# One expert's first layer begun between attention blocks, and a ring of 15 weight slots in place of 13

## The chip, the cores and the metric

The kernel runs on one core of a Trainium2 chip. The metric is device time in microseconds (us) of the whole kernel; less is better. TensorE (PE) does the matrix products, VectorE (DVE), ScalarE (ACT) and GpSimd (POOL) the element work, and SyncE (SP) issues most of the transfers.

## The reference

An attention of 8 heads (local, masked to a band, plus one on sequences averaged by four), then a mixture of 4 dense experts, then one of 8 experts of which each row takes one:

```python
out_up = np.repeat(out_d, factor, axis=2)                 # attention on averaged q, k, v
out_local = np.matmul(attn, v)                            # banded attention, |i - j| < 4
x = out_up + out_local                                    # 2 x 576 rows of 512

p = domain_probs / (domain_probs.sum(-1, keepdims=True) + 1e-09)
for e in range(4):                                        # dense experts, all 1152 rows
    h = np.maximum(x @ w1[e], 0.0)                        # 512 -> 1024
    out += p[:, e:e + 1] * (h @ w2[e])

expert_idx = np.argmax(logits, axis=1)                    # routed experts
for e in range(8):
    mask = expert_idx == e
    h = np.maximum(x[mask] @ w1[e], 0.0)
    out[mask] = gate_w[mask, None] * (h @ w2[e])
```

## The kernel before, in words

Products are made in two parts of fp32: each weight is split into a high part `wh` (a cast on ACT) and a low part `wl` (a subtraction on DVE), and so are x (`xh`, `xl`) and the hidden layer `hT`. Three matmuls (wh with xh, wh with xl, wl with xh) stand for one product.

**Weights.** The class `Weights` holds the order of all 96 weight tiles (128 x 1024, 512 KB each; a quarter of one expert's w1 or w2). A load (L341, SP's queue) brings a tile into one of a few staging tiles (`raw`), `halves(n)` splits the next n halves of 512 columns (cast L357 on ACT, subtraction L361 on DVE) into a slot of a ring of NSLOT = 13 pairs, and a split tile frees its staging tile for the next load. There are 4 staging tiles up to 480 us; then `late_raw` (4) and two pairs of row blocks of `acc` come to them, which makes 10. Half 0 of a w1 tile holds the parts kk 0 and 1 of the inner dimension, half 1 the parts kk 2 and 3; kk is also the number of the attention unit whose rows of x it meets.

**Attention.** Eight units of two heads each. Units 0 to 3 run alone (0 to about 42 us) in the order of the table `ALONE`: each entry is a step and its delay, so that on every engine steps of several units are interleaved. The steps that matter here: `scores_a`, `scores_b` (L133) and `scores_d` (L150), `exp_*` on ACT, `sum_*` and `scale_*` on DVE and POOL, `turn_*` (transposes L222, L239), `value_a`, `value_b` (L284, the local part) and `value_d` (L271, the averaged part), `add_a`, `add_b` (the two sums x, L299 on DVE), `hi` (xh, L72 on ACT) and `lo` (xl, L318 on DVE). `load_qk` brings k and q of a unit (tile `qk`, three buffers), `load_v` brings two layouts of v (`vg`, averaged, and `vw`, banded; unit 3 has its v in `acc`); `pool_v` sums vg on POOL (L115). Behind `lo` of units 0, 1, 2 one, one and two halves of weights are split.

**First expert.** From about 39 us on, 32 steps take f = 0 to 7 of the hidden layer for two chunks of rows (256 columns in the first): `l1` is 12 matmuls (L473) for one f, its relu is hT (L477 on ACT, L478 on DVE), `l2` is L487. Between the steps units 4 to 7 of the attention run, by the table `BESIDE`. l1 of f = 0 needs xh and xl of units 0 to 3.

**Routed experts.** From about 480 us on. `turn_x` transposes gathered rows and makes gx (L1024, L1025), `layer1` is L1034, `t_half` (L980 transposes, L985 hT on ACT, L986 its low part on DVE), `layer2` L1002 (eight matmuls with the high part of hT, then four with the low one). Each expert is a `body` and, behind a branch on its count of rows, `tiles` (a `small` piece or a further body). Within the body of expert e the calls of `split` split the weights of the expert after it. All engines follow their own instructions in the order of the program; a wait on one of them holds everything behind it there.

## Time and profile before

| | us |
|---|---|
| median of three runs (680.36, 680.80, 685.06) | 680.8 |
| the profiled execution | 676.28 |
| its span, first to last instruction | 674.6 |
| PE busy | 646.6 |
| DVE busy | 345.4 |
| ACT busy | 254.3 |
| POOL busy | 105.5 |
| mean granted clock of PE | 0.992 |

The busy time of an engine is the sum of its instructions; PE's share is the one near the span. Rows of the trace give the start of an instruction from the start of the span, how long it took, engine, line, operation, the tile that it writes and those that it reads, and in brackets how long the engine had stood still before it and for what. Lines are those of the kernel before.

### The profile page before, as it was taken

The page shows a single profiled execution, that of the slowest core. Times are in us where ns is not written, and L with a number is a line of the kernel's source. Part 1 is how long each engine was busy: PE and PEld are TensorE (multiplying, and loading weights), DVE is VectorE, ACT ScalarE, POOL GpSimd, SP SyncE. Part 2 cuts the span into 40 slices and gives each one's busy share as a digit, 9 for nine tenths or more (in the row PEclk, how much of TensorE's full clock was granted, in tenths as well). Part 3 has the DMA queues.
Part 4 walks back from the last instruction along what each step waited for, and adds up shares of the span by engine and source line. Part 5 has one row for each costly group of instructions (what it writes and reads, how often), then busy time and mean ns, then how long its engine had stood idle before and what let it go on. Part 6 is the DMA issues. An engine that isn't in the chain of part 4 may idle for free. (4 is left out here: it accounts for less than half of the span.)

```text
span 674.6 us, 11209 instructions
## 1 busy us (share of the span) xinstructions
PE 646.6 (96%) x4203; PEld 569.3 (84%) x4203; DVE 345.4 (51%) x844; ACT 254.3 (38%) x644; POOL 105.5 (16%) x163
## 2 busy tenths in 40 slices
PE   6889999999999999999999999999999989998996
PEld 5677888999999999999999998899899877787875
DVE  6877753214442132342132347977672269498851
ACT  5646542113331111231111234032642367488752
POOL 6725421100000000000000000403031124121211
PEclk9879999999999999999999999999999999999999
DMA  8916500002430011130011138120861166399600
GB/s 229 290 47 214 180 1 2 2 1 62 118 132 2 1 32 32 63 125 0 1 32 62 64 118 248 41 94 0 302 222 57 34 222 225 137 341 360 219 21 30
DMA packets 25500, 73.58 MB, mean 109 GB/s; under 512 B 3102, under 2 KB 6190, under 8 KB 25408
## 3 DMA queue, kind: packets, MB, share of 16 engines
q1 hardware_dynamic: 23104, 66.12, 29.7%
q0 software_dynamic: 2304, 6.33, 2.9%
q8 instruction: 46, 0.75, 0.5%
q14 instruction: 46, 0.38, 0.2%
HBM read 66.13 MB, written 7.09 MB: 109 GB/s over the span
## 5 line engine op out<-in xcount | busy, mean ns | idle before, releaser
L487 PE MATMUL psb<-wh,hT 128*128 128x512 f32 x576 | 198.4, 396 | 0.8 <-DVE hT L478 0.6
L478 DVE SCALAR_TENSOR_TENSOR hT<-psb,hT 128x384 fp32r<-128x384 f32 (+1 forms) x104 | 54.7, 526 | 223.0 <-ACT hT L477 223.0
L477 ACT ACTIVATE hT<-psb 128x384 fp32r<-128x384 f32 (+1 forms) x104 | 48.6, 467 | 288.1 <-PE psb L473 288.1
L473 PE MATMUL psb<-xh,wh 128*128 128x384 f32 (+1 forms) x416 | 137.0, 329 | 1.5 <-ACT xh L72 1.5
L473 PE MATMUL psb<-xl,wh 128*128 128x384 f32 (+1 forms) x416 | 135.7, 326 | 0.4 <-DVE xl L318 0.4
L473 PE MATMUL psb<-xh,wl 128*128 128x384 f32 (+1 forms) x416 | 135.4, 326 | 0.0
L487 PEld LDWEIGHTS psb<-wh,hT 128*128 128x128 f32 x576 | 108.0, 188 | 22.9 <-DVE hT L478 2.0
L487 PE MATMUL psb<-wl,hT 128*128 128x512 f32 x288 | 113.2, 393 | 0.0
L361 DVE TENSOR_TENSOR wl<-raw,wh 128x512 fp32r<-128x512 f32 x132 | 86.1, 700 | 3.9 <-ACT wh L357 3.3
L473 PEld LDWEIGHTS psb<-xh,wh 128*128 128x128 f32 x416 | 78.7, 189 | 6.2 <-ACT xh L72 1.7
L473 PEld LDWEIGHTS psb<-xl,wh 128*128 128x128 f32 x416 | 78.9, 190 | 4.4 <-DVE xl L318 0.6
L473 PEld LDWEIGHTS psb<-xh,wl 128*128 128x128 f32 x416 | 78.8, 189 | 0.0
L357 ACT CAST wh<-raw 128x512 fp32r<-128x512 f32 x132 | 74.4, 624 | 0.1
L487 PEld LDWEIGHTS psb<-wl,hT 128*128 128x128 f32 x288 | 54.1, 188 | 7.7
L1034 PE MATMUL psb<-wh,gx 128*128 128x256 f32 x288 | 58.2, 289 | 0.1
L615 POOL TENSOR_TENSOR rsq<-ss,nr 128x3 f32<-128x3 f32 x9 | 3.3, 370 | 341.9 <-DVE nr L613 323.7
L1002 PE MATMUL psb<-wh,hT 128*128 128x512 f32 x160 | 53.9, 399 | 0.3 <-ACT hT L985 0.3
L1034 PEld LDWEIGHTS psb<-wh,gx 128*128 128x128 f32 x288 | 46.1, 189 | 2.2 <-issue 1.3
L1034 PE MATMUL psb<-wl,gx 128*128 128x256 f32 x144 | 35.9, 283 | 1.1 <-issue 1.1
L1002 PEld LDWEIGHTS psb<-wh,hT 128*128 128x128 f32 x160 | 30.1, 188 | 6.7 <-ACT hT L985 0.5
L1002 PE MATMUL psb<-wl,hT 128*128 128x512 f32 x80 | 31.5, 394 | 0.0
L1034 PEld LDWEIGHTS psb<-wl,gx 128*128 128x128 f32 x144 | 27.2, 189 | 1.7 <-issue 1.3
(245 smaller groups left out, 790.5 us busy)
## 6 DMA issues: line engine op xcount, KB each, us to landing
raw<-in_moe_w_dram SPq DMA_DIRECT2D x66, 512.0 KB
late_raw<-in_moe_w_dram SPq DMA_DIRECT2D x20, 512.0 KB
acc<-in_moe_w_dram SPq DMA_DIRECT2D x10, 512.0 KB
qk<-in_k_dram SPq DMA_DIRECT2D x8, 288.0 KB
qk<-in_q_dram SPq DMA_DIRECT2D x8, 288.0 KB
rows<-acc SPq DMA_DIRECT2D x9, 256.0 KB
vw<-in_v_dram SPq DMA_DIRECT2D x7, 324.0 KB
vg<-in_v_dram SPq DMA_DIRECT2D x7, 288.0 KB
```

Source lines behind the costliest of these rows:

```text
L357: nc.scalar.copy(hi[:, c], t[:, c])
L361: lo_eng.tensor_tensor(lo[:, c], t[:, c], hi[:, c].bitcast(F32), op=ALU.subtract)
L473: nc.tensor.matmul(t, a[:, kk, fs], b_[:, kk, xs], start=(n == 0), stop=(n == 11))
L477: nc.scalar.activation(out=hi, in_=t, func=AF.Relu)
L478: nc.vector.scalar_tensor_tensor(out=lo, in0=t, scalar=0.0, in1=hi.bitcast(F32), op0=ALU.max, op1=ALU.subtract)
L487: nc.tensor.matmul(ys[t], a[:, ts], b_[:, f % 2, :], start=(f == 0 and j == 0), stop=(f == 7 and j == 2))
L615: eng.tensor_tensor(t, ss, y, op=ALU.mult)
L1002: nc.tensor.matmul(y, gh[:, f, a], b_[:, f % 2, :], start=(n == 0), stop=(n == 23))
L1034: nc.tensor.matmul(dst, a[:, kk], w[:, kk, :], start=(n == 0), stop=(n == 11))
```

## The change

Four things. The loads of k, q of unit 3 go to staging tiles 2 and 3 of the ring and stand at the head of SP's queue, ahead of v of unit 1; v of unit 2 and the first two weights are issued at `pool_v` of unit 0, the next two at `scores_d` of unit 3. The first expert's order of weights begins with w1 c0, w1 c1, w2 c0, w2 c1, and behind `lo` of units 0, 1, 2 one, two and one halves are split. `l1_ahead` opens four tiles (f = 0 to 3) between `value_a` and `value_d` of unit 3 with the parts kk 0 and 1, adds kk 2 behind `value_b`, and `l1` of f = 0 to 3 is left with kk 3. And late in the kernel two more slots come to the ring in place of the four `late_raw` tiles (15 slots, 6 staging tiles), four halves are split ahead of the loop over the routed experts, and the bodies of experts 3 and 4 split 14 halves in place of 16.

```diff
--- before.py
+++ after.py
@@ -75,10 +75,13 @@
 
     def load_qk(self, u, d):
         b, hp = self.units[u]
-        t = self.ld.tile([128, 2, S], F32, tag="qk", name="qk", bufs=3)
-        self.nc.sync.dma_start(out=t[:, 1, :], in_=self.k[b, hp])
-        self.nc.sync.dma_start(out=t[:, 0, :], in_=self.q[b, hp])
-        d["qT"], d["kT"] = t[:, 0, :], t[:, 1, :]
+        if "qk" in self.room.get(u, {}):
+            d["qT"], d["kT"] = self.room[u]["qk"]
+        else:
+            t = self.ld.tile([128, 2, S], F32, tag="qk", name="qk", bufs=3)
+            d["qT"], d["kT"] = t[:, 0, :], t[:, 1, :]
+        self.nc.sync.dma_start(out=d["kT"], in_=self.k[b, hp])
+        self.nc.sync.dma_start(out=d["qT"], in_=self.q[b, hp])
 
     def load_v(self, u, d):
         b, hp = self.units[u]
@@ -331,6 +334,7 @@
         self.index = {key: i for i, key in enumerate(order)}
         self.loaded = self.split = self.half = 0
         self.raws = {}
+        self.grown = 1 << 30
 
     def load_to(self, n):
         while self.loaded < min(n, len(self.order)) and self.raw:
@@ -351,7 +355,7 @@
                 return
             self.load_to(i + 1)
             t = self.raws[i]
-            hi, lo = self.slots[i % NSLOT]
+            hi, lo = self.slot(i)
             c = slice(512 * s, 512 * s + 512)
             if hi_engines[self.half % len(hi_engines)] == "a":
                 nc.scalar.copy(hi[:, c], t[:, c])
@@ -375,8 +379,21 @@
 
     def get(self, key):
         i = self.index[key]
-        assert (self.half + 1) // 2 - NSLOT <= i < self.split, (key, i, self.half)
-        return self.slots[i % NSLOT]
+        assert (self.half + 1) // 2 - len(self.slots) <= i < self.split, (key, i, self.half)
+        return self.slot(i)
+
+    def slot(self, i):
+
+        if i < self.grown:
+            return self.slots[i % NSLOT]
+        n = len(self.slots) - NSLOT
+        r = (i - self.grown) % len(self.slots)
+        return self.slots[NSLOT + r] if r < n else self.slots[(self.grown + r - n) % NSLOT]
+
+    def more_slots(self, slots):
+        assert self.half % 2 == 0
+        self.grown = self.half // 2
+        self.slots += slots
 
 
 def rsqrt(nc, pool, y, ss):
@@ -427,7 +444,9 @@
     srcs = [(w1a[e], w2a[e]) for e in range(E1)] + [(w1b[e], w2b[e]) for e in range(E2)]
     order = []
     for e in range(E1):
-        for c in range(4):
+        if e == 0:
+            order += [(0, w, c) for w in (0, 1) for c in (0, 1)]
+        for c in range(2 if e == 0 else 0, 4):
             order += [(e, 0, c), (e, 1, c)]
     for e in range(E1, E1 + E2):
         order += [(e, 0, c) for c in range(4)] + [(e, 1, c) for c in range(4)]
@@ -461,8 +480,27 @@
         if fill:
             fill.pop(0)()
 
+    opened = {}
+
+    def l1_ahead(fs, kks):
+
+        for f in fs:
+            if f not in opened:
+                opened[f] = bank()[:, 0:256]
+            wh, wl = (t.rearrange("p (k f) -> p k f", k=4) for t in W.get((0, 0, f // 2)))
+            fs_ = slice(128 * (f % 2), 128 * (f % 2) + 128)
+            for kk in kks:
+                for j, (a, b_) in enumerate(((wh, xh), (wh, xl), (wl, xh))):
+                    nc.tensor.matmul(
+                        opened[f], a[:, kk, fs_], b_[:, kk, 0:256],
+                        start=(kk == 0 and j == 0), stop=(kk == 3 and j == 2),
+                    )
+
     def l1(e, c, f):
         t0, nt = CHUNKS[e][c]
+        if e == 0 and c == 0 and f in opened:
+            l1_ahead((f,), (3,))
+            return l1_keep(opened.pop(f), f, nt)
         wh, wl = (t.rearrange("p (k f) -> p k f", k=4) for t in W.get((e, 0, f // 2)))
         fs = slice(128 * (f % 2), 128 * (f % 2) + 128)
         xs = slice(128 * t0, 128 * (t0 + nt))
@@ -473,6 +511,9 @@
                 nc.tensor.matmul(t, a[:, kk, fs], b_[:, kk, xs], start=(n == 0), stop=(n == 11))
                 n += 1
                 between()
+        l1_keep(t, f, nt)
+
+    def l1_keep(t, f, nt):
         hi, lo = hT[:, f % 4, 0, 0:128 * nt], hT[:, f % 4, 1, 0:128 * nt]
         nc.scalar.activation(out=hi, in_=t, func=AF.Relu)
         nc.vector.scalar_tensor_tensor(out=lo, in0=t, scalar=0.0, in1=hi.bitcast(F32), op0=ALU.max, op1=ALU.subtract)
@@ -518,20 +559,29 @@
             nc.gpsimd.memset(t[:, 144:160], 0.0)
         acc_f = acc[0:72].rearrange("p t d -> p (t d)")
         pT = acc_f[:, 2304:4608].rearrange("p (n i c) -> p n i c", n=2, i=9)
-        room = {3: dict(vw=acc_f[:, 0:1152], vg=acc_f[:, 1152:2176])}
+        room = {3: dict(qk=[raws[i][:, 0:S] for i in (2, 3)], vw=acc_f[:, 0:1152], vg=acc_f[:, 1152:2176])}
         att = Attention(nc, cst, ld, wk, bank, q, k, v, xh, xl, [pT[:, i] for i in range(2)], room)
         nc.gpsimd.dma_start(out=pr, in_=probs.rearrange("(t p) e -> p t e", p=128))
         half = H // 2
         W.ahead = 0
-        for name, u in (("load_qk", 0), ("load_qk", 1), ("load_qk", 2), ("load_v", 0), ("load_v", 1)):
-            att.load(name, u)
+        for u in range(3):
+            att.load("load_qk", u)
+        att.load("load_v", 0)
+        att.load("load_qk", 3)
+        att.load("load_v", 1)
+        att.load("load_v", 3)
         for name, u in att.run(att.ALONE, range(half)):
-            if name == "scores_d" and u == 0:
-                for name, u in (("load_qk", 3), ("load_v", 3), ("load_v", 2)):
-                    att.load(name, u)
+            if name == "pool_v" and u == 0:
+                att.load("load_v", 2)
+                W.load_to(2)
+            elif name == "scores_d" and u == 3:
                 W.load_to(NRAW)
             elif name == "lo" and u < 3:
-                W.halves((1, 1, 2)[u], "a", "v")
+                W.halves((1, 2, 1)[u], "a", "v")
+                if u == 2:
+                    l1_ahead(range(4), (0, 1))
+            elif name == "value_b" and u == 3:
+                l1_ahead(range(4), (2,))
         W.ahead = NRAW
         run = att.run(att.BESIDE, range(half, 2 * half))
         rest, done = half * len(att.BESIDE), 2
@@ -968,7 +1018,7 @@
     hs_s = lp.tile([128, FF], F32, name="hs_s")
     yo_s = lp.tile([64, DM], F32, name="yo_s")
     yt_s = lp.tile([64, DM], F32, name="yt_s")
-    raws = [lp.tile([128, 1024], F32, name=f"late_raw{i}") for i in range(4)]
+    W.more_slots(make_slots(lp, 2, NSLOT))
 
     def t_half(h, hs2=None):
 
@@ -1065,10 +1115,10 @@
         deliver()
         split(2)
         layer1(e, 1)
-        split(3)
+        split(2 if e in (3, 4) else 3)
         layer1(e, 2)
         t_half(0)
-        split(3)
+        split(2 if e in (3, 4) else 3)
         layer1(e, 3)
         turn_x()
         layer2(e, 0)
@@ -1176,7 +1226,6 @@
     fixed["ab"] = [bank(), bank()]
     for t in range(3):
         r.store(t)
-    W.more_raw(raws)
     layer1(0, 0)
     for t in range(3):
         r.turn(t)
@@ -1217,6 +1266,7 @@
     load_count(0)
     turn_x()
     fixed["h"][2:] = [bank(), bank()]
+    W.halves(4, HI, LO)
     for e in range(E2):
         if e == 1:
             body_ahead(e)
```

On PE, at the end of the attention units that run alone, before the change: value_a of unit 3 (rows with `acc` alone), value_d, value_b, then l1 of f = 0.

```order
L284 MATMUL psb<-acc 64x64 x8
L271 MATMUL psb<-dT,vd 64x144 x4
L284 MATMUL psb<-acc 64x64 x10
L473 MATMUL psb<-xh,wh_92 128x256
L473 MATMUL psb<-xl,wh_92 128x256
L473 MATMUL psb<-xh,wl_93 128x256
```

And now, where wh_92 is the tile of f = 0 and 1, and wh_94 that of f = 2 and 3:

```order
L287 MATMUL psb<-acc 64x64 x8
L494 MATMUL psb<-xh,wh_92 128x256
L494 MATMUL psb<-xl,wh_92 128x256
L494 MATMUL psb<-xh,wl_93 128x256
...
L494 MATMUL psb<-xh,wh_94 128x256
L494 MATMUL psb<-xl,wh_94 128x256
L494 MATMUL psb<-xh,wl_95 128x256
L274 MATMUL psb<-dT,vd 64x144 x4
L287 MATMUL psb<-acc 64x64 x10
L494 MATMUL psb<-xh,wh_92 128x256
```

24 matmuls of the first layer moved in between value_a and value_d, and 12 begin behind value_b.

On SP's queue, behind k and q of units 0, 1, 2 and v of unit 0, before the change (first vg and vw are of unit 1, `acc` is v of unit 3, the last of unit 2):

```order
L90 DMA vg<-in_v_dram 72x1024
L95 DMA vw<-in_v_dram 72x1152
L79 DMA qk<-in_k_dram 128x576
L80 DMA qk<-in_q_dram 128x576
L90 DMA acc<-in_v_dram 72x1024
L95 DMA acc<-in_v_dram 72x1152
```

And now:

```order
L83 DMA raw_111<-in_k_dram 128x576
L84 DMA raw_110<-in_q_dram 128x576
L93 DMA vg<-in_v_dram 72x1024
L98 DMA vw<-in_v_dram 72x1152
L93 DMA acc<-in_v_dram 72x1024
L98 DMA acc<-in_v_dram 72x1152
```

k and q of unit 3 moved ahead of v of unit 1.

On DVE, ahead of the first branch of the routed experts (L1154 before, L1204 now), before the change and then now:

```order
L1025 TENSOR_TENSOR gx<-psb,gx 128x4x128
L1018 CAST gx<-gx 128x4x64
L1154 COMPARE_AND_BRANCH
L1159 COMPARE_AND_BRANCH
L1132 CAST oidx_s<-meta_t 64x1
```

```order
L1075 TENSOR_TENSOR gx<-psb,gx 128x4x128
L1068 CAST gx<-gx 128x4x64
L365 TENSOR_TENSOR wl_101<-raw_109,wh_100 128x512 x2
L365 TENSOR_TENSOR wl_103<-raw_110,wh_102 128x512 x2
L1204 COMPARE_AND_BRANCH
```

Four subtractions came in ahead of the branch; on ACT four casts stand behind its gx in the same way.

## Rows read from the trace of the kernel before

**Rows 1.** The page: span, busy time, share and instructions of each engine.
```profile
span 674.6 us, 11209 instructions
PE 646.6 (96%) x4203; PEld 569.3 (84%) x4203; DVE 345.4 (51%) x844; ACT 254.3 (38%) x644; POOL 105.5 (16%) x163
```

**Rows 2.** Waits of PE: who for whom; us in total, times, longest.
```profile
PE psb L133 <- DMA qk<-in_q_dram: 2.7, 2, 1.7
PE psb L271 <- ACT dT L72: 1.8, 2, 1.1
```

**Rows 3.** Windows: busy us of PE, PEld, DVE, ACT, POOL; PEclk, DMA share, GB/s.
```profile
19.00:24.00 5.00, 5.00 (x83) 4.03 (x84) 4.40 (x14) 3.14 (x17) 3.64 (x7) 1.00 1.03 252
28.00:32.00 4.00, 3.98 (x37) 3.16 (x39) 3.86 (x11) 4.00 (x17) 1.32 (x2) 0.60 0.89 335
42.16:63.24 21.08, 20.27 (x182) 16.06 (x182) 14.95 (x35) 9.97 (x42) 6.11 (x7) 0.84 0.52 159
```

**Rows 4.** Timeline, 18 to 25 us: start, duration, instruction, idle time before it.
```profile
18.88 0.75 DVE L108 TENSOR_REDUCE qd<-qk 128x144 f32<-128x576 f32 x1 [0.18 <-DMA qk<-in_q_dram]
18.99 0.71 PE L133 MATMUL psb<-qk 64*64 64x68 f32 x16 [1.73 <-DMA qk<-in_q_dram]
23.03 0.53 DVE L202 TENSOR_REDUCE sm<-P 128x5 f32<-128x360 f32 x1 [0.39 <-ACT P L175]
24.98 0.26 DVE L195 TENSOR_SCALAR smd<-smd 128x3 f32<-128x3 f32 x1 [0.99 <-ACT Pd L175]
```

**Rows 5.** Timeline, 35 to 43 us.
```profile
35.53 1.15 DVE L361 TENSOR_TENSOR wl<-raw,wh 128x512 fp32r<-128x512 f32 x1
37.45 0.69 PE L284 MATMUL psb<-acc 68*64 68x64 f32 x16
39.40 1.29 DVE L361 TENSOR_TENSOR wl<-raw,wh 128x512 fp32r<-128x512 f32 x2
40.60 0.82 DVE L299 TENSOR_TENSOR x<-psb,od 128x256 f32<-128x256 f32 x2
42.18 0.38 PE L473 MATMUL psb<-xh,wh 128*128 128x256 f32 x1 [1.45 <-ACT xh L72]
```

**Rows 6.** Timeline of PE: first-layer matmuls, six apart, then ten apart.
```profile
47.57 0.41 PE L473 MATMUL psb<-xh,wl 128*128 128x256 f32 x1
48.85 0.41 PE L473 MATMUL psb<-xh,wl 128*128 128x256 f32 x1
...
57.95 0.28 PE L473 MATMUL psb<-xl,wh 128*128 128x256 f32 x1
59.14 0.28 PE L473 MATMUL psb<-xh,wl 128*128 128x256 f32 x1
```

**Rows 7.** Timeline, 50 to 64 us.
```profile
50.16 0.42 DVE L478 SCALAR_TENSOR_TENSOR hT<-psb,hT 128x256 fp32r<-128x256 f32 x1 [1.72 <-ACT hT L477]
63.29 0.52 PE L239 MATMUL psb<-ident,Pd 128*72 128x128 f32 x3 [0.43 <-DVE hT L478]
```

**Rows 8.** Timeline, 503 to 508 us, and four casts in a run at 614 us.
```profile
503.60 0.58 ACT L1024 CAST gx<-psb 128x512 fp32r<-128x512 f32 x1 [1.07 <-PE psb L1022]
505.43 0.29 DVE L1018 CAST gx<-gx 128x256 fp32r<-128x256 f32 x1
506.04 0.39 PE L1002 MATMUL psb<-wh,hT 128*128 128x512 f32 x1
507.90 1.09 PE L1002 MATMUL psb<-wh,hT 128*128 128x512 f32 x4
...
614.15 2.19 ACT L357 CAST wh<-late_raw 128x512 fp32r<-128x512 f32 x4
```

**Rows 9.** Timeline of PE: where a routed expert's work begins behind a branch.
```profile
598.32 0.63 PE L980 MATMUL psb<-ident,acc 128*128 128x128 f32 x4 [0.71 <-DVEq L1154]
664.77 0.63 PE L980 MATMUL psb<-ident,acc 128*128 128x128 f32 x4 [0.30 <-DVE metap L1226]
```

**Rows 10.** Windows, columns as in rows 3: 40 us of the routed experts.
```profile
590.00:630.00 40.00, 36.89 (x242) 32.18 (x241) 35.37 (x73) 32.54 (x68) 7.47 (x6) 1.00 0.96 348
```

## The prediction

> **What bounds the kernel now.** The page's first rows: TensorE (PE) is busy 646.6 of 674.6 us [rows 1], so time is won only where PE stands still, runs at a low clock, or does less. The list of PE's waits says where it stands still; the waits near this change are 2.7 us for q by DMA (the longest 1.7) and 1.8 us for dT from ScalarE (ACT; the longest 1.1) [rows 2]. The windows give the clock: from 42.16 to 63.24 us the granted clock is 0.84 in the mean; as there are two levels, 1.2 and 2.4 GHz, that is 21.08 x 0.16 / 0.5 = 6.7 us at the lower one [rows 3]. The timeline joins the two: PE stands still for 1.45 us until 42.18, for xh of unit 3 [rows 5], and then works at half clock. A first-layer matmul comes every (48.85 - 47.57) / 6 = 0.213 us there, and every (59.14 - 57.95) / 10 = 0.119 us at full clock [rows 6]. So the change works on two stalls (18.99 and 42.18) and on the slow stretch behind the second; it also puts work ahead of the first routed expert (504 us) and takes some from two later ones (584 to 612 us).
>
> **The head: k, q of unit 3 earlier.** PE waits 1.73 us at 18.99 for q of unit 3, VectorE (DVE) 0.18 us at 18.88 for the same q [rows 4]. On SP's queue k3 and q3 now stand ahead of vg1 and vw1 (72 x 1024 and 72 x 1152 elements of 4 bytes, 0.63 MB), at 252 GB/s [rows 3] 2.5 us. So q3 should land at 18.9 - 2.5 = 16.4, before PE asks for it at 18.99 - 1.73 = 17.26. PE's wait goes. But DVE is nearly without a gap there, and can win its own idle time: 0.18, 0.39 at 23.03 and 0.99 at 24.98, sum 1.56 [rows 4]. Against that stands vg1. Before, vw1, k3 and q3 (0.92 MB, 3.7 us) landed behind it, so it was there at about 15.2; now k3 and q3 (0.59 MB, 2.3 us) come first, so 17.5, and GpSimd (POOL) began its sum over vg1 at 17.21: 0.3 to 0.4 us late, with little slack (busy 3.64 of 5.00 us [rows 3]). I take 1.56 - 0.36 = **-1.2 us**, between -0.2 (vg1, and vg2 behind it, set the pace) and -1.7 (all of PE's wait). The weight loads behind them move by less than 1 us and are cast much later: nothing.
>
> **Tiles ahead: the first expert's first step.** 24 matmuls now stand between the local part of unit 3 (value_a) and its downsampled part (value_d), 12 more behind value_b, and 3 are left in each of the steps f0 to f3, where there were 12. PE's work is the same in all.
> Step by step: value_a ends at 38.14 (37.45 + 0.69 [rows 5]); 24 x 0.119 = 2.9 us bring the start of value_d to 41.0 and the end of value_b, 1.3 us on, to 42.3. The two sums x of unit 3 began at 40.60 and took 0.82 [rows 5]; now the second needs value_b, and ends at about 42.85. xh on ACT (0.67) ends at 43.55 and xl on DVE begins at 43.6, where it began at 42.16: **1.4 us later**. PE meanwhile has its 12 matmuls, 42.3 + 1.4 = 43.7: it isn't idle when xh arrives, so the 1.45 us stall goes; about 0.6 us (43.55 + 0.12 to 44.35) are left for xl. The clock should stay at its upper level: an idle time of 1.73 us at 18.99 was followed by 1.00 from 19 to 24 [rows 3, 4], one of 1.45 us at 42.18 by the slow stretch, so a gap of 0.6 us is a likely pass, no certain one.
> What PE could win by 63 us: 27 matmuls fewer (36 before, less the 9 that it ran early, 3.2 us), and half of 6.7 us (3.4), less 1.4: about 5 us. But DVE has the chain that PE waits for: from xl of unit 3 to hT of f3, 42.16 to 63.24, it is busy 14.95 of 21.08 us [rows 3], and at 63.29 PE waits 0.43 us for that hT [rows 7]. DVE's work there stays the same, for the same number of halves is split before it. From 43.6 on, 14.95 us end at 58.55; to that comes the idle time that is left. Of 6.13 us idle, 1.72 (50.16) came from a PE at half clock [rows 7] and should go, with some 0.4 more of that kind; the rest waits for ACT's exponentials and casts, which start earlier but don't get shorter. I keep 2.0 us: 60.55 against 63.24, **-2.7 us**. If only 2.1 go: 62.6, -0.7; if 0.5 is left: 59.05, -4.2. From 64 to 480 us PE stands still for less than 1 us, so what it has won by then moves the end.
> Held banks: four PSUM banks stay open until f3, so the next output tile of PE shares a bank with unit 4's exponentials on ACT and waits for them. The cover is PE's own lead of 2 us over DVE; I cost it at nothing (without the cover, one group of exponentials, 1.2 us).
> The split half that moves from the third unit to the second lands beside POOL's work. DVE's row at 35.53, beside POOL, took 1.15 us; two at 39.40 took 1.29 together, 0.65 each [rows 5]: +0.5 us of DVE, hidden, as PE's 24 matmuls begin 1.4 us after it. The Trainium skill, GPSIMD Engine Reference, section 1. Specifications, says that GpSimd shares its SBUF interfaces with VectorE and contends with DVE instructions that have two SBUF inputs: it speaks against this place, and the trace agrees, with 1.15 against 0.65 us. Put on the path, it would take 0.5 us off the gain.
>
> **The ring: 15 slots, six staging tiles.** Four halves now stand on ACT and DVE between the last turn of x and the first branch. Four casts take 2.19 us [rows 8]. ACT's gx ends at 504.18 and hT came right behind; now hT starts at 506.4, its first part (0.35) ends at 506.7, and the second layer begins there instead of at 506.04, +0.7. DVE has its cast of gx until 505.72, then four subtractions, 4 x 0.645 = 2.58 us, so 508.3; two copies and the first hT (0.7) end at 509.0, where the low matmuls began at 507.90 [rows 8]: **+1.2 us** with the hand-over. The cover would be other work for PE ahead of this layer, and the order has none. Between 0 and +2.6 (all of DVE's share).
> Experts 3 and 4 split 14 halves where they split 16: 1.1 us less on ACT and 1.3 on DVE in each. PE waits 0.71 us at such a boundary (598.32) for DVE, and 0.30 at the last one (664.77), where the body before split 8 halves [rows 9]. So at most 0.4 a body; I take **-0.4** for both, between 0 and -0.8.
> Staging tiles: 6 instead of 10. The DMA engines run at 0.96 and 348 GB/s from 590 to 630 us [rows 10]; a weight of 128 x 1024 x 4 bytes takes 1.5 us. A body of 13.7 us uses 8 weights, 12 us of DMA, in bursts of one per 1.2 us; six tiles, full at its start, last for it. I cost it at nothing.
>
> **Sum.** -1.2 - 2.7 + 1.2 - 0.4 = -3.1 us. The profiled execution is 676.28 us (span 674.6 [rows 1] and 1.7 around it), so 673.2. It lies 4.5 us under the median of the runs shown, 680.8; against that median the forecast is **677.7 us**.
>
> **Rivals.**
> 1. DVE doesn't hold the gain back. Head -1.7, steps -4.2, ring 0, bodies -0.4: -6.3, **674.5 us**. For it: 6.13 us of idle time in DVE's chain [rows 3]. Against it: most of that waits for ACT, not for PE.
> 2. The clock falls again. PE is ahead of DVE by about 2 us in f0 to f3, so it idles there in gaps, and a gap of 1.1 us (dT [rows 2], just ahead of 28) was followed by 0.60 from 28 to 32 [rows 3]. A low stretch as long as before costs 3.4 us and eats the 2.7: -1.2 + 0.8 = -0.4, **680.4 us**. The Trainium skill, TensorE: Matmul & The Clock Gate, A second HAM failure mode: psum-queue depth-cycling, says that frequent short idle times between groups of matmuls send the clock down and up: by it the gain of the steps would be lost. The trace is divided: 1.73 us of idle time passed at 18.99, 1.45 did not at 42.18.
> 3. The other side: staging tiles. Bodies of experts 3 to 6, 584 to 640 us: six tiles are used up within a body, ACT stands at a cast with hT behind it in its queue, and PE behind hT. Price: 1.5 us for each weight that comes late. One in each of four bodies is +6.0, less 3.1: **683.7 us**; it decides from the third late weight on. For it: DMA at 0.96 [rows 10] has nothing to spare when 8 weights and the gathers are wanted in 13.7 us. Against it: two of the four bodies want a weight less, and with ten tiles no cast waited for a load.
>
> **How the numbers follow.** Forecast (675.8 to 679.5): 0.45. Rival 1: 0.17. Rival 2: 0.25. Rival 3: 0.13. The range, 673.5 to 682.0, reaches past the middle of rival 1 and over rival 2, and leaves out most of rival 3. One per cent, 6.8 us, is about what a measurement of this kernel can tell from no change: faster than 674.0 takes the far part of rival 1, 0.10; slower than 687.6 wants two late weights a body, 0.04; within 1%: 0.86.
>
> **What would show it.** Right: no PE wait for q near 17 to 19 us; PE's wait for xh near 43 under 0.5 us, and the clock at 1.00 from 40 to 62; hT of f3 3 to 4.5 us before 63.24 (head and steps); the second layer of the first routed body 2 to 3 us behind gx; no ACT wait for a DMA past 580 us. Wrong: a clock under 0.9 in 40 to 62, POOL waiting over 1 us for vg near 17, ACT casts that wait for a load in the routed experts.

## The result, and the profile after

| | before | after |
|---|---|---|
| median of the runs taken side by side (20 each), us | 679.97 | 684.48 |
| ratio after / before, 95% interval | | 1.0063, 1.0043 to 1.0083 |
| profiled execution, us | 676.28 | 688.9 |

The changed kernel is slower, by about 4.3 us (0.0063 x 680). The forecast was 677.7 us, the range 673.5 to 682.0. The loss is small, 0.6 per cent, but clear of the noise: the interval leaves out 1.

The first rows of the page after, which answer to [rows 1]:

```profile
span 687.1 us, 11208 instructions
PE 657.9 (96%) x4203; PEld 577.9 (84%) x4203; DVE 347.1 (51%) x844; ACT 255.4 (37%) x644; POOL 100.0 (15%) x163
```

PE does the same 4203 matmuls and is busy 11.3 us longer, so more of its work ran at the lower clock. This is not what separates the medians: the mean granted clock is 0.987 over the 20 executions of the changed kernel and 0.988 over 29 of the kernel before, a difference worth some 0.7 us (0.001 x 680). The profiled execution of after (clock 0.977) is the slowest of its 20. Of the waits of [rows 2] the one for q fell from 2.7 to 0.9 us (its longest part, of 1.7, is gone); the one for dT grew from 1.8 to 2.7 us:

```profile
PE psb L274 <- ACT dT L72: 2.7, 2, 1.6
```

The windows of after (columns as in [rows 3]) show where in the attention part the clock is low:

```profile
34.00:45.00 11.00, 9.85 (x72) 8.15 (x73) 7.11 (x13) 4.70 (x11) 5.27 (x7) 0.54 0.08 30
45.00:60.00 15.00, 14.59 (x180) 11.73 (x178) 8.93 (x25) 7.72 (x29) 1.86 (x3) 1.00 0.39 125
```

In this execution the slow stretch did not go; it moved. Before, it lay behind 42.18 us [rows 3, 5]; now it lies at 34 to 45 us (0.54), ahead of and under the tiles begun early. Two rows of the kernel before (start, duration, engine, line, operation, tiles, idle time ahead of it), then the timeline of after, 32 to 50 us:

```profile
34.19 0.72 PE L271 MATMUL psb<-dT,vd 72*64 72x144 f32 x8 [0.65 <-ACT dT L72]
42.16 0.76 DVE L318 TENSOR_TENSOR xl<-x,xh 128x576 fp32r<-128x576 f32 x1 [0.74 <-ACT xh L72]
```

```profile
32.47 1.09 DVE L198 TENSOR_SCALAR smd<-smd 128x3 f32<-128x3 f32 x1
34.39 0.87 DVE L74 COPY acc<-psb 68x128 f32<-68x128 f32 x2
34.70 0.40 ACT L72 COPY dT<-psb 72x288 f32<-72x288 f32 x1 [2.55 <-DVE acc L74]
35.15 1.23 PE L274 MATMUL psb<-dT,vd 72*64 72x144 f32 x8 [1.61 <-ACT dT L72]
41.07 1.12 PE L287 MATMUL psb<-acc 68*64 68x64 f32 x16
42.12 0.58 PE L494 MATMUL psb<-xh,wh 128*128 128x256 f32 x1
46.26 0.28 PE L494 MATMUL psb<-xh,wl 128*128 128x256 f32 x1
47.61 0.82 DVE L302 TENSOR_TENSOR x<-psb,od 128x256 f32<-128x256 f32 x2 [4.35 <-ACT od L72]
49.18 0.76 DVE L321 TENSOR_TENSOR xl<-x,xh 128x576 fp32r<-128x576 f32 x1 [0.74 <-ACT xh L72]
```

Read from the top: PE waits 1.61 us for dT, where it waited 0.65 before; ACT's dT itself stands 2.55 us behind a copy on DVE. PE then goes on at half clock: value_a of unit 3 ends at 42.19 (forecast 38.14), the 24 matmuls of the tiles ahead stand between 42.12 and 46.54, and DVE has nothing to do for 4.35 us until the sums x can start. xl of unit 3 begins at 49.18; it began at 42.16 before, and 43.6 was forecast.

The timeline of after, 65 to 74 us, where four tiles are closed:

```profile
65.16 0.42 DVE L519 SCALAR_TENSOR_TENSOR hT<-psb,hT 128x256 fp32r<-128x256 f32 x1
65.77 1.27 POOL L118 TENSOR_TENSOR pv<-vg 72x512 f32<-72x512 f32 x1 [4.72 <-DMA vg<-in_v_dram]
67.80 0.91 POOL L212 TENSOR_TENSOR Pd<-Pd,smd 128x432 f32<-128x432 f32 x1
68.76 1.32 PE L242 MATMUL psb<-ident,Pd 128*72 128x128 f32 x6 [1.95 <-POOL Pd L212]
73.11 0.42 DVE L519 SCALAR_TENSOR_TENSOR hT<-psb,hT 128x256 fp32r<-128x256 f32 x1 [1.02 <-ACT hT L518]
```

The first and the last row are hT of f = 3 and f = 4. In the kernel before they are:

```profile
62.83 0.41 DVE L478 SCALAR_TENSOR_TENSOR hT<-psb,hT 128x256 fp32r<-128x256 f32 x1
67.55 0.41 DVE L478 SCALAR_TENSOR_TENSOR hT<-psb,hT 128x256 fp32r<-128x256 f32 x1
```

Between them lie 7.95 us instead of 4.72: POOL waits 4.72 us for vg of unit 4, then scales Pd, and PE waits 1.95 us for Pd (where it waited 0.43 us for DVE [rows 7]). This wait is nowhere in the prediction. Last, two rows of after from the routed experts:

```profile
515.36 0.50 PE L1052 MATMUL psb<-wh,hT 128*128 128x512 f32 x1 [0.38 <-ACT hT L1035]
577.35 1.14 ACT L361 CAST wh<-raw 128x512 fp32r<-128x512 f32 x2 [0.54 <-DMA raw<-in_moe_w_dram]
```

PE waits behind the four halves, as forecast, and a cast waits for its load, as rival 3 said.

### The profile page after: what moved, and what is told of

The parts are those of the page before. It is cut to its first block, busy times and chain, and to the rows that moved or that the text cites. A ratio compares the mean times of both kernels' runs of the same rounds, so it can differ in the third digit from the quotient of the medians.

```text
span 687.1 us, 11208 instructions
## 1 busy us (share of the span) xinstructions
PE 657.9 (96%) x4203; PEld 577.9 (84%) x4203; DVE 347.1 (51%) x844; ACT 255.4 (37%) x644; POOL 100.0 (15%) x163
## 5 line engine op out<-in xcount | busy, mean ns | idle before, releaser
L511 PE MATMUL psb<-xh,wh 128*128 128x384 f32 (+1 forms) x400 | 132.0, 330 | 0.0
L511 PE MATMUL psb<-xl,wh 128*128 128x384 f32 (+1 forms) x400 | 130.8, 327 | 0.0
L511 PE MATMUL psb<-xh,wl 128*128 128x384 f32 (+1 forms) x400 | 130.8, 327 | 0.0
L365 DVE TENSOR_TENSOR wl<-raw,wh 128x512 fp32r<-128x512 f32 x160 | 105.5, 711 | 7.6 <-ACT wh L361 6.7
L361 ACT CAST wh<-raw 128x512 fp32r<-128x512 f32 x160 | 89.4, 624 | 0.6 <-DMA raw<-in_moe_w_dram 0.5
L511 PEld LDWEIGHTS psb<-xh,wh 128*128 128x128 f32 x400 | 75.7, 189 | 4.3 <-issue 0.2
L511 PEld LDWEIGHTS psb<-xl,wh 128*128 128x128 f32 x400 | 75.7, 189 | 3.8
L511 PEld LDWEIGHTS psb<-xh,wl 128*128 128x128 f32 x400 | 75.7, 189 | 0.0
L1084 PE MATMUL psb<-wh,gx 128*128 128x256 f32 x288 | 60.5, 296 | 0.2
L1084 PEld LDWEIGHTS psb<-wh,gx 128*128 128x128 f32 x288 | 47.8, 195 | 2.3 <-issue 1.4
```

The lines of the kernel that those rows point to most:

```text
L361: nc.scalar.copy(hi[:, c], t[:, c])
L365: lo_eng.tensor_tensor(lo[:, c], t[:, c], hi[:, c].bitcast(F32), op=ALU.subtract)
L511: nc.tensor.matmul(t, a[:, kk, fs], b_[:, kk, xs], start=(n == 0), stop=(n == 11))
L1084: nc.tensor.matmul(dst, a[:, kk], w[:, kk, :], start=(n == 0), stop=(n == 11))
```

## The experiments

Each kernel was timed in rounds beside the kernel before, except where noted. Below, "us" beside a ratio is (ratio - 1) x 680.

| kernel | ratio to before, 95% interval | us |
|---|---|---|
| a_only: attention part alone | 1.0038, 1.0011 to 1.0065 | +2.6 |
| b_only: ring part alone | 1.0053, 1.0027 to 1.0079 | +3.6 |
| behind: changed, all early tiles behind value_b | 1.0081, 1.0055 to 1.0107 | +5.5 |
| raw6: six staging tiles alone | 1.0033, 1.0004 to 1.0063 | +2.2 |
| dve_extra: four subtractions done twice | 1.0044, 1.0017 to 1.0071 | +3.0 |
| act_scale: row maxima scaled on ACT | 1.0000, 0.9967 to 1.0032 | 0.0 |
| head_only: loads of k, q of unit 3 first | 1.0005, 0.9975 to 1.0036 | +0.3 |
| ahead_only: early tiles alone | 1.0008, 0.9974 to 1.0041 | +0.5 |
| behind_only: early tiles alone, behind value_b | 1.0035, 1.0004 to 1.0067 | +2.4 |
| fill2: two tiles, behind value_b | 1.0007, 0.9989 to 1.0024 | +0.5 |
| order_only: the order of weights alone | 0.9991, 0.9964 to 1.0019 | -0.6 |
| qk7_before: load order of unit 7 alone | 1.0005, 0.9978 to 1.0032 | +0.3 |
| qk7_a_only | 0.9993, 0.9973 to 1.0013 | -0.5 |
| qk7_after | 1.0047, 1.0024 to 1.0071 | +3.2 |
| qk7_fill2 | 0.9958, 0.9936 to 0.9981 | -2.9 |
| k8_a_only | 0.9986, 0.9959 to 1.0013 | -1.0 |
| k8_fill2 | 0.9954, 0.9923 to 0.9986 | -3.1 |

### The two parts apart, the early tiles moved, and the changed kernel once more

a_only undoes the ring part, b_only the attention part (the four edits of the diff split where the change lists them). `behind` moves the 24 early matmuls:

```diff
-                if u == 2:
-                    l1_ahead(range(4), (0, 1))
             elif name == "value_b" and u == 3:
-                l1_ahead(range(4), (2,))
+                l1_ahead(range(4), (0, 1, 2))
```

> The attention part alone (head loads, order of weights, tiles ahead), with the ring of 13 slots and 10 staging tiles and the splits as before. Theory 1 (24 matmuls ahead of value_d hold up the sums x of unit 3; VectorE idles there some 4 us and is the bound up to about 90 us): slower than before by 2 to 4 us. Theory 2 (the loss comes from the ring and the four halves at 504 us): faster than before by 2 to 4 us, as forecast. Theory 3 (the clock): the time follows the granted clock, 0.98 and less where it is slow.

> The ring part alone (15 slots, six staging tiles, four halves ahead of the routed experts, 14 halves in two bodies), with the attention as before. Theory 1: slower by 0.8 to 2 us, the price put on it in the prediction. Theory 2: slower by 4 us and more. Theory 3: within 1 us of before, as the clock of the first 80 us is that of before.

> The changed kernel, but all 36 matmuls ahead (parts 0, 1 and 2 of four tiles) stand behind value_b of unit 3 and none ahead of value_d. Theory 1: the sums x of unit 3 come as early as before, VectorE has no gap of 4 us, and the kernel is 3 to 5 us faster than the changed one: 0 to 2 us faster than before. Theory 2: as slow as the changed kernel, +4 us. Theory 3: between the two, as the clock falls.

> The changed kernel once more, for a second profile. Theory 1: VectorE again stands idle for about 3 to 4 us ahead of the sums x of unit 3, at whatever clock, and TensorE waits over 1 us for VectorE or GpSimd between 60 and 72 us. Theory 3: the gaps are there only where the clock is at its lower level.

Both parts cost. `again`, the changed kernel executed once more, took 682.27 us (span 680.5, clock 0.987). There, too, DVE stands idle ahead of the sums x of unit 3, with the clock at 1.00 (2.12 us, the row below; nothing before), and PE waits 1.70 us for Pd at 64.90. Behind value_b the early tiles are no cheaper, so their place between value_a and value_d alone does not explain the loss.

```profile
44.02 0.82 DVE L302 TENSOR_TENSOR x<-psb,od 128x256 f32<-128x256 f32 x2 [2.12 <-ACT od L72]
```

What the prediction had taken for a property of the kernel shows in b_only, whose attention part is that of before. The windows from xl of unit 3 to hT of f = 4, each by its own times, of before, b_only, a_only (in this order):

```profile
42.16:67.55 25.39, 24.53 (x213) 19.98 (x214) 18.18 (x43) 13.82 (x56) 8.88 (x11) 0.87 0.55 172
```
```profile
42.22:65.61 23.39, 21.34 (x210) 17.43 (x211) 17.98 (x43) 13.82 (x56) 8.82 (x11) 1.00 0.66 189
```
```profile
46.29:69.13 22.84, 18.23 (x185) 14.28 (x185) 18.24 (x44) 13.93 (x56) 8.79 (x11) 1.00 0.65 191
```

The same stretch in the same order ran at 0.87 in one execution and at 1.00 in another, and was 2.0 us shorter there. With the early tiles it is 0.55 us shorter again, no more: DVE has some 18 us of work in it in all three. And it begins 4.1 us later in a_only. Not all of the four are the price of the early tiles, since xl also comes late without them where the clock fell ahead of it (44.18 in raw6, whose attention is that of before, and 45.08 in order_only). Compared at an equal time at the lower clock ahead of 110 us (3.4 us, one execution each), PE's matmul that starts at 110 us in before comes 1.6 us earlier in b_only and 2.0 earlier in qk7_before, both with the old order of first loads and tiles, but only 0.1 earlier in k8_a_only, which has the early tiles (the qk7 and k8 kernels are described below). At 10.3 us of lower clock before and raw6 stand at 0 and +1.1, again, ahead_only and qk7_after at +1.9, +2.6 and +3.6. So the early tiles bought 0.5 to 1.3 us behind xl, paid some 3 ahead of it in k8_a_only (45.37 against 42.22), and lost 1.5 us or more: near the 2.6 us that a_only measured, but read from single executions.

Four rows of b_only (hT of f = 3 and f = 4, POOL's sum over vg of unit 4, PE's first matmul with Pd) hold two more things:

```profile
59.83 0.41 DVE L517 SCALAR_TENSOR_TENSOR hT<-psb,hT 128x256 fp32r<-128x256 f32 x1
65.61 0.41 DVE L517 SCALAR_TENSOR_TENSOR hT<-psb,hT 128x256 fp32r<-128x256 f32 x1
58.06 1.29 POOL L118 TENSOR_TENSOR pv<-vg 72x512 f32<-72x512 f32 x1 [3.12 <-DMA vg<-in_v_dram]
61.41 0.85 PE L242 MATMUL psb<-ident,Pd 128*72 128x128 f32 x6 [1.63 <-POOL Pd L212]
```

With the attention of before, hT of f = 3 ends here at 60.24, earlier than the 60.55 that was forecast of the changed kernel. And POOL's wait for vg is there without any early tile: it was hidden in the profiled execution of before, whose DVE came later.

### The ring part: which of its edits costs

raw6 is the kernel before with six staging tiles in place of ten, and nothing else:

```diff
-    raws = [lp.tile([128, 1024], F32, name=f"late_raw{i}") for i in range(4)]
...
-    W.more_raw(raws)
```

> The kernel before with its four late staging tiles left out: six instead of ten, and nothing else. If staging tiles are what the ring part costs (rival 3): slower by 2 to 3.6 us, with ACT casts or TensorE waits later than before in the routed experts. If its cost is the four halves at 504 us and the new order behind them: within 0.7 us of before.

It costs 2.2 of the part's 3.6 us. Its timeline (ACT, ACT, PE):

```profile
571.22 0.62 ACT L357 CAST wh<-raw 128x512 fp32r<-128x512 f32 x1 [1.67 <-DMA raw<-in_moe_w_dram]
571.74 0.64 ACT L984 CAST hT<-psb 128x256 fp32r<-128x256 f32 x2
572.16 0.50 PE L1001 MATMUL psb<-wh,hT 128*128 128x512 f32 x1 [0.86 <-ACT hT L984]
```

ACT stands at a cast whose load has not landed, hT stands behind it in ACT's queue, and PE waits for hT. Lining up PE's matmuls of the two kernels, raw6 falls 1.4 us back from 570 to 579 us and another 1.0 by 669. In the kernel before no cast waits for a load in this stretch. The other kernels say how much such a comparison of two executions is worth: from 560 to 581 us of the kernel before, the thirteen others with ten staging tiles lie within 0.3 us of it, and the five with the whole ring part fall 0.5 to 1.1 back (2.6 in qk7_after, with a stretch at the lower clock). From 499 to 507 us, where the four halves stand, those five lose 0.7 to 0.9 us (b_only 0.9), all others 0.0 or less. In the four of them that were executed more than once the time is also 0.2 to 0.4 us longer outside the span from first to last instruction, and no trace shows why.

### DVE's load, and the head alone

dve_extra repeats the subtraction of four halves on DVE (halves 8 to 11 of the order); act_scale takes the scaling of the row maxima (TENSOR_SCALAR, x -scale) from DVE and multiplies on ACT; head_only makes only the edit to the first loads.

```diff
-            lo_eng.tensor_tensor(lo[:, c], t[:, c], hi[:, c].bitcast(F32), op=ALU.subtract)
+            for _ in range(2 if self.half in (8, 9, 10, 11) else 1):
+                lo_eng.tensor_tensor(lo[:, c], t[:, c], hi[:, c].bitcast(F32), op=ALU.subtract)
```
```diff
-        self.nc.vector.tensor_scalar(out=m, in0=m, scalar1=-scale, scalar2=None, op0=ALU.mult)
+        self.nc.scalar.mul(d["mx"][:, 0:4], d["mx"][:, 0:4], -0.125)
...
+        self.nc.scalar.mul(d["mx"][:, 4:9], d["mx"][:, 4:9], -0.125)
...
+        self.nc.scalar.mul(d["mxd"], d["mxd"], -0.125 / 16)
```

> The kernel before with four subtractions wl done twice (halves 8 to 11, 60 to 67 us): 4 x 0.68 = 2.7 us more work on VectorE, the same result. Theory D (VectorE is the bound there): slower by 2 to 3 us. If TensorE is the bound there, as the prediction had it behind 64 us: within 0.7 us of before.

> The kernel before, with the scaling of the row maxima (24 small instructions on VectorE, 0.17 us each alone, 0.4 to 1.9 us beside GpSimd's work; 7.9 us in all) moved to ScalarE, just ahead of the exponentials. Theory D: faster by 2 to 5 us, as VectorE loses 7.9 us in the first 112 us. If TensorE is the bound: within 1 us of before.

> Only the head of the change: k, q of unit 3 at the head of SP's queue (and the loads behind them moved with them); weights, tiles and ring as before. Theory D (VectorE, held up by GpSimd, sets the pace from 17 to 78 us): TensorE's wait of 1.7 us at 19 us goes, comes back as a wait of over 2 us for dT near 34 us, and the kernel is within 1 us of before. The prediction's step: 1.2 us faster. Theory C (the idle time near 34 us lowers the clock): 1 to 2 us slower, with a mean clock lower by 0.002 or more.

2.6 us more of DVE cost 3.0 us (0.0017 x 680 = 1.2 at the least), though PE's rows line up with a loss of only 0.8 of it from 59 to 71 us, where the work was added, and the profiled execution was at the lower clock for some 19 us more than that of before (0.978 of 686.4 us, 0.992 of 674.6); it agrees with a DVE that sets the pace and settles nothing. act_scale moves nothing measurable, against the 2 to 5 us of theory D (beside GpSimd's work these instructions took 0.3 to 1.3 us in before, not up to 1.9). The head gains nothing measurable either. Its timeline:

```profile
18.05 0.71 PE L136 MATMUL psb<-raw,raw 64*64 64x68 f32 x16
26.41 2.13 DVE L162 TENSOR_SCALAR mx<-mx 128x5 f32<-128x5 f32 x1
34.32 0.88 DVE L74 COPY acc<-psb 68x128 f32<-68x128 f32 x2
35.08 1.24 PE L274 MATMUL psb<-dT,vd 72*64 72x144 f32 x8 [2.08 <-ACT dT L72]
```

PE's wait for q is gone, as forecast (first row; [rows 4] has 1.73 us). But DVE did not win its idle time: a scaling of five columns now falls beside a sum on POOL and takes 2.13 us (0.72 before, at 26.94; 0.83 in after), and DVE's copy of unit 2 comes at 34.32, later than the 33.43 of before. PE, early, waits the longer for dT. What sets the time of that copy shows in the sums of POOL over v of unit 2, of before and of after:

```profile
23.95 1.26 POOL L115 TENSOR_TENSOR pv<-vg 72x512 f32<-72x512 f32 x1 [0.47 <-DMA vg<-in_v_dram]
24.90 1.27 POOL L118 TENSOR_TENSOR pv<-vg 72x512 f32<-72x512 f32 x1 [0.92 <-DMA vg<-in_v_dram]
```

From the start of this sum to DVE's copy lie 9.5 us in both (33.43 and 34.39), in head_only (24.84 to 34.32) and in twelve other traces, to within 0.02 us. So POOL, which has waited for v in most of them, paces this stretch, and DVE follows. The new loads bring PE there earlier, and POOL not: in head_only and after its sum starts 0.9 us later than before, in `again` 0.4 earlier.

### The attention part's edits apart

```diff
             elif name == "value_b" and u == 3:
+                l1_ahead(range(2), (0, 1, 2))
```

That is fill2: of f = 0 and 1 the parts kk 0 to 2 stand behind value_b, 18 matmuls where 9 stood. ahead_only has the early tiles as changed but no new first loads; behind_only the same with all of them behind value_b; order_only only the order of the weights and no early tile.

> Only the tiles ahead, with the order of weights that they need (head loads and ring as before): 24 matmuls ahead of value_d of unit 3, 12 behind value_b. The prediction's step: 2.7 us faster. Theory D (VectorE sets the pace from 17 to 78 us, and these matmuls make the sums x of unit 3 some 3 us late): 1.5 to 3 us slower.

> As ahead_only, but all 36 matmuls stand behind value_b of unit 3. The sums x are in time, the first relu is 1.5 to 2 us later than before. Theory D: 0.5 to 2 us slower, less than ahead_only. The prediction's sum with nothing late on VectorE: 2.7 us faster or more.

> The kernel before, with 18 matmuls (parts 0, 1, 2 of f = 0 and 1, for which its own order of weights is enough) behind value_b of unit 3: 9 that stood there already, and 9 that fill most of TensorE's 1.45 us wait at 42 us. Nothing on VectorE is later than before, and the second relu comes earlier. Theory D: 0 to 1.5 us faster, as VectorE's wait of 1.7 us at 50 us shrinks. If idle time at 42 us is what lowers the clock: also a higher mean clock by 0.002.

> Only the order of the first expert's weights and the halves behind lo of units 0, 1, 2 (1, 2, 1 in place of 1, 1, 2), without tiles ahead. The moved subtraction lands beside GpSimd's work (1.15 us in place of 0.65). Theory D: 0 to 0.7 us slower. If the order itself is the loss: 2 us slower and more.

None gains, and their intervals overlap, so these runs do not tell which edit of the attention part costs. Common to the traces with early tiles is what after showed: POOL waits 4.3 us (ahead_only), 4.5 (behind_only), 5.4 (fill2) for vg of unit 4, where it waited 1.34 before. It waits less, but does wait, without early tiles: 3.1 us in b_only and head_only, 3.2 in order_only, nothing in raw6.

### SP's queue: where the wait for vg comes from

The waits of SP, 20 to 75 us (who for whom; us in total, times, longest), of before, then of after:

```profile
SPq L79 <- DVE qd L108: 16.8, 1, 16.8
```
```profile
SPq L83 <- DVE qd L111: 22.0, 1, 22.0
```

SP stands at the load of k of unit 7. Its buffer is that of unit 4, and is free when DVE has averaged q of unit 4 (qd; the expectations below name the scores of unit 4, which read the buffer too, but the last to let go is qd). Behind it in SP's queue stand three weights and v of unit 4; the DMA engines have nothing to do (share 0.08 at 34 to 45 us in after, above). So whatever delays qd of unit 4, the early tiles among it, delays the load that unit 4 waits for. The same two loads in before, after, and in a_only with the new order:

```profile
47.13 0.33 SPq L79 DMA_DIRECT2D qk<-in_k_dram  x1
49.40 0.40 SPq L90 DMA_DIRECT2D vg<-in_v_dram  x1
```
```profile
52.94 0.33 SPq L83 DMA_DIRECT2D qk<-in_k_dram  x1
55.21 0.41 SPq L93 DMA_DIRECT2D vg<-in_v_dram  x1
```
```profile
36.98 15.13 SPq L351 DMA_DIRECT2D raw<-in_moe_w_dram  x3
52.15 0.39 SPq L96 DMA_DIRECT2D vg<-in_v_dram  x1
```

The new order, here in four kernels, issues k and q of unit 7 behind v of unit 4:

```diff
     def load_qk(self, u, d):
+        if u == 7 and 4 not in self.have_v:
+            return
...
     def load_v(self, u, d):
...
+        self.have_v.add(u)
+        if u == 4:
+            self.load_qk(7, self.st.setdefault(7, {}))
```

> The kernel before with one transfer order changed: k and q of unit 7 are issued behind v of unit 4 instead of ahead of three weight loads and that v. Theory S (SP stands at k of unit 7, whose buffer is held until the scores of unit 4 are done, and v of unit 4 waits behind it): the DMA engines' idle stretch from about 36 to 47 us goes, vg of unit 4 lands before GpSimd wants it (58.93 us before, 1.34 us of waiting), PE's wait for Pd of unit 4 (0.43 us at 63.29 before) goes; 1 to 2 us less in all. Rival (PE's pace to 65 us is set by DVE's chain alone, whatever vg does): no change, within 0.5 us.

> The attention part of the change alone, with k and q of unit 7 issued behind v of unit 4. Theory S: without it this part costs 2.6 us, as vg of unit 4 comes 3 us later and PE waits 2.55 us at 64.92 for Pd; with it the wait goes and the part gains what was forecast of it, 1 to 3 us under the kernel before. Rival: still about 2.6 us over.

> The changed kernel with k and q of unit 7 issued behind v of unit 4. Theory S: the attention part no longer costs, the ring part (2.5 us alone) stays: between 1 us under and 2.5 us over the kernel before, against 4.2 over without the new order. Rival: about 4.2 us over, as without it.

> The kernel before with nine matmuls of the first layer (f = 0 and 1, kk 0 to 2) doubled in effect behind value_b as cover, which cost 0.3 us (no change) and moved PE's wait for Pd to 3.75 us at 65.03; and with k and q of unit 7 issued behind v of unit 4. Theory S: that wait goes, 1.5 to 3 us under the kernel before. Rival: no change.

(In qk7_fill2 nothing is doubled: the nine matmuls of f = 1 are moved up. The 0.43 us at 63.29 before were a wait for hT of DVE [rows 7], not for Pd. The ring part alone is 3.6 us in the table, not 2.5.) In qk7_a_only vg is hardly issued earlier (52.15; 52.33 in a_only); it lands earlier, since two weights went in the idle stretch and k, q no longer stand ahead of it. The rows of a_only, then of qk7_a_only:

```profile
61.60 1.26 POOL L118 TENSOR_TENSOR pv<-vg 72x512 f32<-72x512 f32 x1 [3.44 <-DMA vg<-in_v_dram]
64.92 0.85 PE L242 MATMUL psb<-ident,Pd 128*72 128x128 f32 x6 [2.55 <-POOL Pd L212]
```
```profile
58.16 1.28 POOL L124 TENSOR_TENSOR pv<-vg 72x512 f32<-72x512 f32 x1
64.17 0.52 PE L248 MATMUL psb<-ident,Pd 128*72 128x128 f32 x3 [0.92 <-DVE hT L525]
```

POOL no longer waits, and PE waits for DVE again. From hT of f = 3 to f = 4 it is 4.74 us in qk7_a_only and 4.73 in qk7_after (4.72 before; 5.79 in a_only, 7.95 in after). Part of what is won there is lost again ahead of f = 3, which comes 17.38 us behind xl in qk7_after and 15.98 in after; from xl to f = 4 it is 22.11 against 23.93, and 22.57 in `again`. The times follow in two of four: fill2 goes from +0.5 to -2.9 us with disjoint intervals, though with a higher mean clock (0.990, and 0.986 in the kernel before beside it), and a_only from +2.6 to -0.5, with intervals that just overlap. The kernel before does not change (+0.3, where 1 to 2 us less were forecast), although b_only's execution has the wait in the same order. qk7_after stays at +3.2, not told apart from the changed kernel's +4.3: the ring part's cost is in it. So the wait for vg is shown, and that the new order removes it; what it is worth in the median is shown for fill2 alone. The forecast of 1 to 3 us under the kernel before for qk7_a_only was missed.

### The copy that dT stands behind

ACT's second copy into dT reads a bank of PSUM that DVE's copy keep_8 reads too, and starts when that is done. The last two kernels move keep_8:

```diff
     def keep_8(self, u, d):
-        self.copy("v", d["pT"][0:68, 8, :], d["p2"][0][0:68, 384:512])
+        self.copy("a", d["pT"][0:68, 8, :], d["p2"][0][0:68, 384:512])
```

> The attention part alone, k and q of unit 7 behind v of unit 4, and one copy of each unit (keep_8, 68 x 128 from PSUM into pT) on ScalarE instead of VectorE. Theory K: ScalarE's copy into dT reads the same bank as keep_8 and stands behind it (2.42 us at 34.01 in the kernel without this edit); keep_8 stands in VectorE's queue behind a row operation of three columns that takes 1.08 us beside GpSimd, and so PE waits 2.55 us at 34.45 and the clock falls for the tiles ahead. With keep_8 on ScalarE the second dT starts about 1.3 to 2 us earlier, PE's wait at 34 to 35 is under 1 us, and the kernel is 0.5 to 2.5 us under the one without the edit (which measured 0.9993 of the kernel before). Rival (VectorE's own chain sets 65 us whatever PE does): within 0.5 us of it.

> The kernel before with k and q of unit 7 behind v of unit 4, the first layer's parts kk 0 to 2 of f = 0 and 1 (18 matmuls, of which 9 stood there before) between value_b of unit 3 and the next unit, and keep_8 on ScalarE. Theory K: PE's wait of 1.92 us at 34.97 falls under 1 us, and the kernel is 0.5 to 2.5 us under the one without the edit (0.9958 of the kernel before). Rival: within 0.5 us of it, since VectorE paces the units up to 46 us.

Rows of qk7_a_only, then of k8_a_only (`acc` holds pT):

```profile
34.01 0.40 ACT L73 COPY dT<-psb 72x288 f32<-72x288 f32 x1 [2.42 <-DVE acc L75]
34.45 1.24 PE L280 MATMUL psb<-dT,vd 72*64 72x144 f32 x8 [2.55 <-ACT dT L73]
```
```profile
31.72 0.34 ACT L73 COPY acc<-psb 68x128 f32<-68x128 f32 x1
31.88 0.48 ACT L73 COPY dT<-psb 72x288 f32<-72x288 f32 x1
32.41 0.72 PE L280 MATMUL psb<-dT,vd 72*64 72x144 f32 x8 [0.19 <-ACT dT L73]
45.37 0.76 DVE L327 TENSOR_TENSOR xl<-x,xh 128x576 fp32r<-128x576 f32 x1 [0.74 <-ACT xh L73]
```

dT comes 2.1 us earlier and PE's wait is gone: the mechanism is right. The price was wrong: xl of unit 3 comes only 0.95 us earlier (46.32 to 45.37), and the ratios, 0.9986 against 0.9993 and 0.9954 against 0.9958, lie within each other's intervals. In k8_a_only PE then waits for POOL (0.93 us at 34.61 for P, 0.56 at 35.48 for Pd). PE's lead is not worth much here, as the rival said. k8_fill2 has the lowest median of the study, 676.35 us beside 679.38 of before, not told apart from qk7_fill2.

## Why the prediction was wrong

- **What it started from.** It took the slow stretch of 42 to 63 us [rows 3] for a property of the kernel and counted half of its 6.7 us as there to be won. b_only, in the same order, has a clock of 1.00 there and needs 2.0 us less; its hT of f = 3 ends at 60.24 without any early tile, ahead of the forecast 60.55. So most of the gain against 63.24 was there to be had without the change. This is the step that failed first: one execution's clock was priced as the kernel's.
- **Head, -1.2.** Measured +0.3 (-1.7 to +2.4). The landing of q was right, and POOL's slack by vg too (0.42 us of waiting at 18.54 in after). Wrong was that DVE wins 1.56 us of idle time less 0.36: POOL's sum over v of unit 2 sets its pace up to 34 us, the case to which the prediction gave -0.2; in head_only its short operations fell beside POOL's sums and were held (2.13 us for one).
- **Early tiles, -2.7.** The step "1.4 us later" failed: xl of unit 3 began 3.4 us later than before in `again` (45.58) and 7.0 later in after (49.18). One part of it is the 24 matmuls ahead of value_d, which leave DVE idle for 2.1 us (`again`) to 4.4 us (after). The other is "value_a ends at 38.14": PE's wait for dT, 0.65 us before, was 1.6 to 2.9 us in the kernels with the new first loads (0.19 once keep_8 was moved), and the clock fell beside it. Not all of that wait comes from the change: raw6, with the attention part of before, had 1.97 us there and a slow clock behind it, order_only 1.62, b_only 0.46. DVE's chain took what was forecast: 14.95 + 2.0 = 16.95 us from xl to the end of hT of f = 3; from 49.18 to 65.16 + 0.42, 16.40 us, was measured. But at a clock of 1.00 the old order takes 18.02 (b_only), so the early tiles shorten it by 1.6, where the forecast took 4.1 off the 21.08 of a slow execution.
- **Behind f = 3.** The prediction let what was won by 63 us move the end, since PE stands still for less than 1 us from 64 to 480. It didn't look at what unit 4 waits for: SP's queue. Between f = 3 and f = 4 after needs 3.2 us more than before (7.95 against 4.72), but 1.1 of them are in b_only too (5.78), and part of the rest is the lower clock (0.78 from 64 to 70 us). With the new order it is 4.7.
- **Four halves, +1.2.** Right in place, somewhat high: 0.7 to 0.9 us in the five kernels that have them.
- **Bodies of 3 and 4, -0.4.** Right in sign and place: lined up with before, b_only wins 0.6 us between 581 and 613. 0.8 us is lost again behind it, by 629.
- **Staging tiles, 0.** Wrong: 2.2 us (0.3 to 4.3). Six tiles full at the start of a body were said to last for it, for a body that takes 8 weights; the first that starved was expert 2's, whose body splits 18 halves, 9 weights, ahead of the ones that rival 3 named. In raw6 the casts at 598 and 612 us, in those, wait 0.6 and 0.4 us.
- **The rivals.** Rival 3's mechanism, given 0.13, is the larger part of the ring part's loss, at about a third of the price that was asked of it (2.2 of 6.0); that its 683.7 us lies near the measured 684.5 is luck, as it counts the forecast gain of 3.1 in. Rival 2 was right that the clock falls again, in another place than it named; but over the executions the mean clock is that of before to within 0.001, so such falls carry some 0.7 of the 4.3 us at the most. Rival 1's condition (DVE doesn't hold the gain back) is contradicted: some 18 us of DVE stand from xl to f = 4 in before, b_only and a_only.

The ring part's loss is shown by its own run and located in the traces. Open is which edit of the attention part makes its 2.6 us (0.7 to 4.4), as head_only, ahead_only and order_only show nothing by themselves, and why qk7_after keeps +3.2. That the two parts together (+4.3, 2.9 to 5.6) cost less than their sum (+6.2) is within the intervals, 2 us either way each.

## What to carry over

Ahead of filling a stall on one engine, follow each in-order queue, the one that issues transfers too, past that place: a load that waits for a buffer holds every load behind it (16.8 us here), and work that fills the stall can delay the buffer. Price a slow-clock stretch only if a second execution shows it in the same place. Count staging tiles against the body that takes most weights: the sum here took eight, and the one that starved takes nine.

## What the runs showed of the hardware

A short DVE operation can be held until an operation on POOL ends. In after, the scaling at 32.47 of three columns took 1.09 us and ended at 33.56; POOL's sum over v of unit 3 ran from 32.26 to 33.53. The same operation for another unit took 0.26 at 24.98 before [rows 4], beside a sum on POOL that was near its end (25.21), and 1.26 at 24.93 in after, beside one that had just begun (24.90 to 26.17). The Trainium skill, SBUF — State Buffer, SBUF: two separate sides, calls the port pair that GpSimd shares with some DVE operations an exclusive lock, held for a whole instruction, and not a division of bandwidth. The trace agrees: 1.09, 0.26 and 1.26 us, each ending within 0.03 us of POOL's sum.

The clock fell to its lower level at the end of a PE wait of 1.61 us (after, low from 34.8 to 45.0 us) and behind two of 0.93 and 0.56 us (k8_a_only, low from 37.2 to 40.6), and not behind one of 1.73 us in the kernel before [rows 3, 4]. The length of the wait ahead does not tell by itself whether it falls.
